# First batch of a Fourier filter followed by an MLP mixer: length-47 steps as four 64x64 tiles, results put back and transposed on chip

## The chip, the cores and the metric

The kernel runs on one core of a Trainium2 chip. The metric is the device time of one execution in microseconds (us). Engines are named as in the profile: PE is the matrix engine (PEld its weight loads), DVE the vector engine, ACT the scalar engine, POOL the GpSimd engine, SP the engine whose instruction queue only issues transfers here. ACT and POOL issue transfers too. Ln is line n of the kernel before unless the changed kernel is named.

## The reference, cut to what matters

```python
# x: (8, 3008, 256) f32; filt_r, filt_i: (1505, 256); weights arrive as 64-bit floats
X = np.fft.rfft(x, axis=1)
y = np.fft.irfft(X * (filt_r + 1j * filt_i)[None], n=3008, axis=1)      # "the filter"
h = np.maximum(y.transpose(0, 2, 1) @ w_tok1, 0) @ w_tok2               # 3008 -> 256 -> 3008
u = y + h.transpose(0, 2, 1)
out = u + np.maximum(u @ w_ch1, 0) @ w_ch2                              # 256 -> 1536 -> 256
```

## The kernel before, in words

**The transform.** 3008 is 47 x 64. A transform of the sequence is a length-64 step along one index (`wa`, a 128x128 matmul on 24 folded rows, `a_unit`, L533), a length-47 step for each of 32 frequencies k2 (`wb`, 96 rows in, 128 out), the product with the filter, the length-47 step back (`wi`) and the length-64 step back, which is part of the mixer's own matmul (`u_filter`, L872). Between the length-64 step and the length-47 step the data must be transposed: what lay on partitions (k2 and one of four parts g) has to lie in the free dimension, and the 24 rows a have to lie on partitions.

**The batches.** The eight batches are filtered one after the other, each beside the mixer of the batch before it, in steps placed by hand. Batches 1 to 7 transpose by writing to DRAM (`z_tmp`) and reading back, do the length-47 step as four 64x64 tiles of the PE array (`b_sets`, `bi_sets`, whose matmuls go through the helper `four`, L525), and write the result to DRAM again (`g_tmp`, L726), from which the mixer loads it (`t4_load`, L781). None of this has a mixer to lie beside in the first batch, so batch 0 is built otherwise:

- The length-64 step (12 matmuls, L535) is copied by ACT into one tile `turned`, a run of 256 channels for each of 32 places, and 16 DVE transposes in 32x32 blocks (L653), each over 16 channels, turn it in place. An element's neighbour in such a block lies 256 floats, 1 KB, further.
- For each of the 32 frequencies, `b_unit` (L666) does one 128x128 matmul of 256 columns whose stationary is every second column of a table (L668), DVE multiplies the result by the real and the imaginary part of the filter (L673), and `bi_unit` (L676) does two matmuls (L682). ACT copies the result out (L692) and writes it to `g_tmp` from its own queue (L689) for every second frequency. ACT also makes the second half of each filter tile (L253) and of each inverse table (L260, L261).
- The mixer's token product needs all of it: `t4_load` reads `g_tmp` back in pieces (L1270 to L1282, L784), and `token_sums` (L786) does 48 matmuls of 256 columns with the first mixer weight, which lies converted in `w1`.

**Weights beside it.** The weights are 64-bit floats and are converted on chip in tiles: 12 of the first mixer weight (0 to 11, 512 columns), 14 of the second (12 to 25, 470 columns, but 188 in tiles 18 and 25), then those of the channel weights (26 and on). For one tile ACT makes the top part (L281), DVE does four operations (L283 and L284, the first half, in `convert_middle`; L287 and L289, the second half, in `convert_end`), and top and rest are summed into place either by two PE matmuls and an ACT copy (L327, L328, L330: tiles 0 to 11, and the first `BY_PE` = 6 of the second weight) or by DVE (L316, the rest). Three scratch pairs are in use in turn, and `fill` keeps loads five tiles ahead. From step 27 of the 32 no new loads are started until the 32 steps are over (`pause`, L1262).

**Order.** The order on every engine is the order in which the program emits instructions; each engine works its own list in order. The main part (L1241 to L1301) emits the length-64 step, then the 32 steps with half a weight tile in each, so that 16 tiles are converted beside them, then the loads from `g_tmp`, then tiles 16 to 25 with `token_sums` in one piece after tile 17, then a ReLU (L866), two projections (`u_unit`, L879, each followed by a copy, L887) with tiles 26 and 27 beside them, and the sums of `v_steps` (L1298). Then the mixer's loop begins (`mix`, L1125). The channel weights' tile `both` (L1283) takes the memory of `turned`.

Of the kernel before, what the change touches and what calls it, by code (L numbers as in the profile page):

```python
# [37 lines left out]
WC = 2  # L38
TI = P - 2 * KH + 1
# [11 lines left out]
PARTS = (0, 64, 96, 112)  # L51
BY_PE = 6
# [7 lines left out]
def _make_tables():  # L60
# [12 lines left out]
    wa, wai = wa.reshape(P, P), wai.reshape(P, P)  # L73
# [25 lines left out]
    f = np.float32  # L99
    wi = wi.reshape(P, K2, KR)  # L100
    wa0 = wa.reshape(P, K2, 4).transpose(0, 2, 1).reshape(P, P)
    wbi0 = np.zeros((4, K2, K2, P + KR))
    wbi0[:, 0:A, :, 0:P] = wb
    wbi0 = wbi0.reshape(P, K2, P + KR)
    wbi0[:, :, P:] = wi
    places = np.zeros((P, K2, 2 * P))
    places[:, :, 0::2] = wbi0[:, :, 0:P]
    places[:, :, TI:TI + 2 * KR:2] = wbi0[:, :, P:]
    wbi0 = np.concatenate((places[one, :, 0:P], places[two, :, P:]))
    wbi0 = wbi0.reshape(P, K2 // WC, WC, P).transpose(0, 1, 3, 2)  # L110
# [18 lines left out]
def kernel(  # L129
# [26 lines left out]
                 for g, bs in enumerate(GROUPS)] for what, shape in (("z", (P, A)), ("g", (K2, KR))))  # L156
# [57 lines left out]
    turned = turned[:, 0:K2 * D].rearrange("p (s d) -> p s d", d=D)  # L214
# [7 lines left out]
    def filt_quad(c):  # L222
        t = filts[c % FB]
        for i, src in enumerate((filt_r, filt_i)):
            for odd in range(KC):
                k, to = c * KD + odd, odd * HALF
                nc.sync.dma_start(t[to:to + A, i], raw(src, k, [[64 * D, A], [KC * D, 2], [1, D]]))
                down = t[to + 32:to + 32 + A]
                if k:
                    nc.sync.dma_start(down[0:A - 1, i], raw(src, 64 - k, [[64 * D, A - 1], [-KC * D, 2], [1, D]]))  # L230
                else:
                    nc.sync.dma_start(down[:, i, 0], raw(src, 32, [[64 * D, A], [1, D]]))
                    nc.sync.dma_start(down[0:A - 1, i, 1], raw(src, 64 - KC, [[64 * D, A - 1], [1, D]]))

    def filt_load(c):
        t, k0 = filts_0[c % len(filts_0)], c * KC


        q = nc.gpsimd if c != 1 else nc.sync
        for src, i, p0 in ((filt_r, 0, 0), (filt_i, 1, 0)):  # L240
            q.dma_start(t[p0:p0 + A, i], raw(src, k0, [[64 * D, A], [D, KC], [1, D]]))
            lo = p0 + 32
            if k0 == 0:
                q.dma_start(t[lo:lo + A, i, 0, :], raw(src, 32, [[64 * D, A], [1, D]]))
            k = max(k0, 1)

            for j0, n in ((0, 16), (16, A - 1 - 16)):
                q.dma_start(t[lo + j0:lo + j0 + n, i, k - k0:KC, :],
                            raw(src, 64 * (j0 + 1) - k, [[64 * D, n], [-D, k0 + KC - k], [1, D]]))

    def filt_double(c):
        t = filts_0[c % len(filts_0)]
        nc.scalar.copy(out=t[HALF:P], in_=t[0:HALF])  # L253


    turn_i = sp.tile([P, 4, WC, KR], FP32, tag="s", name="turn_i")

    def table_turn(g, wb):
        wi, to = wb[:, TI:TI + 2 * KR:2].rearrange("p r k -> p k r"), turn_i[:, g % 4]
        nc.scalar.copy(out=to[0:HALF], in_=wi[HALF:P])  # L260
        nc.scalar.activation(out=to[HALF:P], in_=wi[0:HALF], func=AF.Copy, scale=-1.0)  # L261
# [40 lines left out]
    def rounded(st, n, parts, late):  # L302
        if late:

            late_in.reverse()
            where, tag = late_in[0]
            both = where.tile([P, 2, 512], FP32, tag=tag, name="both")
            pair = both[:, 0], both[:, 1]
        else:
            pair = spare_pair()  # L310
        h = halves(st, n, pair)
        yield next(h)
        yield next(h)
        top, rest = next(h)
        for src, dst in parts:
            nc.vector.tensor_tensor(out=dst, in0=src(top), in1=src(rest), op=ALU.add)  # L316
# [39 lines left out]
    def w2_load(i):  # L356
# [20 lines left out]
        else:  # L377
            yield from rounded(st, n, parts, False)
# [12 lines left out]
    def wc1_load(i, late=True):  # L391
# [6 lines left out]
        yield from rounded(st, 512, [(lambda v: v.rearrange("p (i j n) -> p i j n", j=2, n=P),  # L398
# [5 lines left out]
    def wc2_load(i):  # L404
# [8 lines left out]
        yield from rounded(st, 512, [(tile_of(dh), chan[1][:, i, n].rearrange("p j (g i) -> p j g i", i=CW))  # L413
# [47 lines left out]
    begun, pause = [0], []  # L461

    def fill(ahead):
        while not pause and begun[0] < len(tiles) and begun[0] < ended[0] + (4 if begun[0] >= len(tiles) - len(LAST) else ahead):
            start()
# [55 lines left out]
    def rows_of(t_d, b):  # L521
        g, i = place_of[b]
        return t_d[g].rearrange("k (g a) b d -> (k g) a b d", a=A)[:, :, i, :]

    def four(outs, stat, mov):  # L525
        for i in range(2):
            for j in range(2):
                nc.tensor.matmul(outs(i, j), stat(i, j), mov(i, j), start=True, stop=True)  # L528
# [4 lines left out]
    def a_unit(b, c):  # L533
        ps = bank(free_bank())
        nc.tensor.matmul(ps, wa0 if b == 0 else wa, xs.pop((b, c)).rearrange("p a d -> p (a d)"), start=True, stop=True)  # L535
        if b == 0:
            d0, c = divmod(c, NXC // 2)
            nc.scalar.copy(out=turned[:, ts(c, 2 * XC), ds(d0 * P, P)], in_=ps.rearrange("p (a d) -> p a d", d=P))
# [27 lines left out]
    def dft(bs):  # L566
# [5 lines left out]
        kept = []  # L572

        def table_load(c):
            if first:
                if c < 5:
                    where, tag = (t1p, "t1") if c > 2 else (wbp, "wb")
                    t = where.tile([P, 2 * P, WC], FP32, tag=tag, name="wb")
                    for h in range(2):
                        nc.gpsimd.memset(t[half_of(h), ts(1 - h, P)], 0.0)  # L580
                    kept.append(t)
                wbs[c] = kept[c % 5]
                for h in range(2):
                    nc.sync.dma_start(wbs[c][half_of(h), ts(h, P)], wbi0_d[half_of(h), c])
            else:
                wbs[c] = wbp.tile([P, 2, 4, HALF], FP32, tag="wb", name="wb")
                nc.sync.dma_start(wbs[c], wbi_d[:, ts(c, 2)])
# [4 lines left out]
        def w_load(c):  # L592
            table_load(c)
            (filt_load if first else filt_quad)(c)
# [45 lines left out]
        for i, u in enumerate(() if tiled else todo):  # L640
            if first and i in (0, 2):
                w_load(i // 2)
            if first and i in (6, 8):
                table_load(i // 2 - 1)
# [4 lines left out]
            if first and (i + 1) % (NXC // 2) == 0:  # L649

                for d in range(i // (NXC // 2) * P, (i + 1) // (NXC // 2) * P, 16):
                    v = turned.rearrange("p s d -> p d s")[:, d:d + 16, :]
                    nc.vector.transpose(v, v)  # L653
        t2s, t3s, prods = {}, {}, {}
# [11 lines left out]
        def b_unit(k):  # L666
            ps = bank("pg").rearrange("p (b d) -> p b d", b=2)[:, 0:nb, :]
            nc.tensor.matmul(ps, wbs[k // WC][:, 0:2 * P:2, k % WC], turned[:, k, :].unsqueeze(1), start=True, stop=True)  # L668
            t = filts_0[k // KC % len(filts_0)]
            if k == 0:  # L670
                prods["all"] = p1p.tile([P, 2, 2, D], FP32, tag="p1", name="p1")
            p1 = prods["all"][:, k % 2]
            nc.vector.tensor_tensor(out=p1, in0=ps.to_broadcast([P, 2, D]), in1=t[:, :, k % KC, :], op=ALU.mult)  # L673
            prods[k] = (p1[:, 0:1], p1[:, 1:2])

        def bi_unit(k):  # L676


            ps = bank(free_bank()).rearrange("p (b d) -> p b d", b=2)[:, 0:nb, :]
            for i, p in enumerate(prods.pop(k)):  # L680
                wi = turn_i[:, k // WC % 4, k % WC] if i else wbs[k // WC][:, TI:TI + 2 * KR:2, k % WC]
                nc.tensor.matmul(ps[0:KR], wi, p, start=(i == 0), stop=(i == 1))  # L682
            c, r = divmod(k, KC)
            if r == 0:
                where, tag = (p2p, "p2") if c % 3 == 2 else (t3p, "t3")
                t3s[c] = where.tile([KR, KC, nb, D], FP32, tag=tag, name="t3")
            by_block(t3s[c][:, r], ps[0:KR])
            if r == KC - 1:
                nc.scalar.dma_start(g_d[0][ts(c, KC)].rearrange("k r b d -> r k b d"), t3s.pop(c))  # L689

# [4 lines left out]
        def two_banks(tags):  # L695
            return [bank(tag).rearrange("p (j d) -> p j d", j=2) for tag in tags]

# [7 lines left out]
        def products(c, pss):  # L705
            where = (p1p, p2p)
            for h in range(2):
                prods[c, h] = where[h].tile([P, 2, 2, D], FP32, tag="p%d" % (h + 1), name="p%d" % (h + 1))
                nc.vector.tensor_tensor(out=prods[c, h], in0=pss[h].unsqueeze(1).to_broadcast([P, 2, 2, D]),
                                        in1=filts[c % FB], op=ALU.mult)  # L710
# [6 lines left out]
        def bi_sets(c, tags):  # L717
# [7 lines left out]
            for h in range(2):  # L725
                nc.sync.dma_start(g_d[place_of[bs[0]][0]][ts(c, KD), ts(h, KH)].rearrange("k r b d -> r k (b d)"),  # L726
                                    t3[half_of(h, KH)])
# [9 lines left out]
        yield "b"  # L737
        if not first:
            last = K2 // KD
# [13 lines left out]
        if first:  # L753
            for i in range(2):
                t = t2p.tile([P, 2, KC, D], FP32, tag="t2", name="filt")
                nc.gpsimd.memset(t[0:HALF], 0.0)
# [613 lines left out]
```

## Time and profile before

| | us |
|---|---|
| median of 3 runs (2404.61 to 2407.17) | 2407.01 |
| the profiled execution, its own time | 2404.98 |
| its span, first to last instruction | 2403.2 |
| last length-64 matmul's copy ends (ACT) | 21.5 |
| in-place transposes (L653) begin, end | 13.9, 31.1 |
| first product with the filter (L673) begins | 32.5 |
| last copy out of the length-47 step (L692) ends | 105.4 |
| token product (L790) begins, last matmul ends | 111.7, 132.7 |
| `v_steps` (L955 on `v`) begins | 139.7 |

What lies outside the span is 2404.98 - 2403.2 = 1.8 us. In the answers of the trace a row of groups has the line, the engine and operation, output<-input with shapes, the count, then the busy time and the mean of one in ns, then the idle time just before and what ended it. Each fp32 matmul has two records, so that x96 are 48 matmuls. In a table of stretches each engine has its busy time and (x) its records; then come the granted PE clock, the busy share of the 16 transfer engines, and what they moved in GB/s.

### The profile page before, as it was taken

The page shows a single profiled execution, that of the slowest core. Times are in us where ns is not written, and L with a number is a line of the kernel's source. Part 1 is how long each engine was busy: PE and PEld are TensorE (multiplying, and loading weights), DVE is VectorE, ACT ScalarE, POOL GpSimd, SP SyncE. Part 2 cuts the span into 40 slices and gives each one's busy share as a digit, 9 for nine tenths or more (in the row PEclk, how much of TensorE's full clock was granted, in tenths as well). Part 3 has the DMA queues.
Part 4 walks back from the last instruction along what each step waited for, and adds up shares of the span by engine and source line. Part 5 has one row for each costly group of instructions (what it writes and reads, how often), then busy time and mean ns, then how long its engine had stood idle before and what let it go on. Part 6 is the DMA issues. An engine that isn't in the chain of part 4 may idle for free.

```text
span 2403.2 us, 37053 instructions
## 1 busy us (share of the span) xinstructions
PE 2359.4 (98%) x13132; PEld 2012.9 (84%) x13132; DVE 1951.0 (81%) x3669; ACT 689.8 (29%) x1339; POOL 638.3 (27%) x1124
## 2 busy tenths in 40 slices
PE   7989999999999999999999999999999999999998
PEld 4667888888898888988888888988889888898887
DVE  7798887788887888788887788778887788877786
ACT  5732222222223222232222222222222322212222
POOL 7477434211211121112112311221121112112121
PEclk8999999999999999999999999999999999999999
DMA  9963546333353333533344333533335433331100
GB/s 218 241 195 121 152 119 226 114 118 85 106 188 124 100 95 117 189 118 96 98 145 158 117 93 103 186 120 107 90 114 172 132 98 98 108 130 32 39 14 21
DMA packets 189719, 294.28 MB, mean 122 GB/s; under 512 B 34444, under 2 KB 124962, under 8 KB 189534
## 3 DMA queue, kind: packets, MB, share of 16 engines
q1 hardware_dynamic: 148046, 231.24, 31.0%
q0 software_dynamic: 34688, 53.83, 8.6%
q10 hardware_dynamic: 6800, 6.85, 0.9%
q8 instruction: 104, 1.70, 0.3%
q14 instruction: 81, 0.66, 0.1%
HBM read 209.06 MB, written 82.72 MB: 121 GB/s over the span
## 4 chain that ended last, share of the span: by engine, by line
PE 92%; DVE 3%; DMA 2%; issue 1%; POOL 1%; ACT 1%; SPq 0%; ACTq 0%; DVEq 0%; POOLq 0%
PE ps_po L1011 35%; PE ps_pg L977 20%; PE ps_pg L993 15%; PE ps_b L528 3%; PE ps_b L841 3%; PE ps_acc L898 3%; PE ps_acc L841 2%; PE ps_pg L528 2%; PE ps_b L898 2%; PE ps_b L876 2%; PE ps_acc L876 2%; DVE both L284 0%; DVE t L955 0%; DMA g_tmp<-t 0%; DVE both L289 0%
## 5 line engine op out<-in xcount | busy, mean ns | idle before, releaser
L1019 POOL DMA_DIRECT2D out_dram<-r x752 | 408.3, 550 | 1452.0 <-issue 1028.0
L998 ACT ACTIVATE hh<-hh 128x512 f32<-128x512 f32 (+1 forms) x576 | 348.0, 621 | 1017.7 <-DVE hh L955 1013.8
L955 DVE TENSOR_TENSOR hh<-ps_pg,s 128x512 f32<-128x512 f32 (+3 forms) x864 | 482.5, 586 | 171.3 <-ACT s L980 161.1
L1011 PE MATMUL ps_po<-t,wc 128*128 128x256 f32 (+1 forms) x2296 | 558.1, 380 | 0.7 <-DVE t L955 0.7
L1011 PEld LDWEIGHTS ps_po<-t,wc 128*128 128x128 f32 x2296 | 427.7, 190 | 95.6 <-issue 38.7
L977 PE MATMUL ps_pg<-v,wc 128*128 128x256 f32 (+1 forms) x1728 | 412.6, 375 | 1.4 <-POOL wc L386 1.4
L1011 PE MATMUL ps_po<-hh,wc 128*128 128x256 f32 (+1 forms) x1722 | 411.5, 375 | 0.6 <-POOL wc L387 0.6
L977 PEld LDWEIGHTS ps_pg<-v,wc 128*128 128x128 f32 x1728 | 327.9, 190 | 39.6 <-POOL wc L386 2.2
L1011 PEld LDWEIGHTS ps_po<-hh,wc 128*128 128x128 f32 x1722 | 326.8, 190 | 38.4 <-POOL wc L387 1.4
L993 PE MATMUL ps_pg<-u,wc 128*128 128x256 f32 (+1 forms) x1152 | 292.3, 376 | 5.7 <-DVE hh L955 5.6
L955 DVE TENSOR_TENSOR t<-t,hh 128x256 f32<-128x256 f32 (+1 forms) x576 | 247.1, 429 | 19.8
L993 PEld LDWEIGHTS ps_pg<-u,wc 128*128 128x128 f32 x1152 | 217.2, 190 | 37.1 <-DVE hh L955 10.8
L955 DVE TENSOR_TENSOR s<-ps_pg,hh 128x512 f32<-128x512 f32 (+1 forms) x288 | 196.1, 681 | 30.0
L980 ACT COPY s<-ps_pg 128x256 f32<-128x256 f32 (+1 forms) x288 | 105.8, 368 | 332.4 <-PE ps_pg L977 329.1
L955 DVE TENSOR_TENSOR t<-hh 128x512 f32<-128x512 f32 (+1 forms) x288 | 194.4, 675 | 0.6 <-ACT hh L998 0.6
L977 PE MATMUL ps_pg<-u,wc 128*128 128x256 f32 (+1 forms) x576 | 169.3, 376 | 3.9 <-DVE hh L955 3.9
L993 PE MATMUL ps_pg<-v,wc 128*128 128x256 f32 (+1 forms) x576 | 169.2, 375 | 0.0
L977 PEld LDWEIGHTS ps_pg<-u,wc 128*128 128x128 f32 x576 | 108.1, 190 | 19.7 <-DVE hh L955 7.5
L993 PEld LDWEIGHTS ps_pg<-v,wc 128*128 128x128 f32 x576 | 109.2, 190 | 13.0
L955 DVE TENSOR_TENSOR u<-ps_acc,u 128x256 f32<-128x256 f32 (+1 forms) x84 | 46.2, 550 | 72.4 <-PE ps_acc L898 50.1
L955 DVE TENSOR_TENSOR u<-ps_b,u 128x512 f32<-128x512 f32 (+2 forms) x126 | 74.5, 591 | 28.8 <-PE ps_b L898 26.7
L898 PE MATMUL ps_acc<-w 128*128 128x256 f32 (+1 forms) x336 | 85.2, 376 | 0.0
(164 smaller groups left out, 2686.8 us busy)
## 6 DMA issues: line engine op xcount, KB each, us to landing
w<-w_tmp SPq DMA_DIRECT2D x84, 448.0 KB
w<-w_tmp SPq DMA_DIRECT2D x35, 896.0 KB
out_dram<-r POOLq DMA_DIRECT2D x696, 32.0 KB, 3.4
g_tmp<-t SPq DMA_DIRECT2D x112, 192.0 KB
t<-g_tmp SPq DMA_DIRECT2D x42, 512.0 KB
t<-z_tmp SPq DMA_DIRECT2D x196, 96.0 KB
z_tmp<-t SPq DMA_DIRECT2D x72, 256.0 KB
wb<-wbi_t SPq DMA_DIRECT2D x56, 256.0 KB
```

Of the source, the lines that this page charges most:

```text
L528: nc.tensor.matmul(outs(i, j), stat(i, j), mov(i, j), start=True, stop=True)
L841: nc.tensor.matmul(ps[:, at], w[:, n], mov, start=(j == 0 and i in (0, 2)), stop=(j == AP - 1 and i >= 5))
L876: nc.tensor.matmul(ps[:, ds(q * P, n)], t4[b, c][:, r, ts(dh, P)], wai[:, 0:n], start=(first and q == 0), stop=(not first and q == 3))
L898: nc.tensor.matmul(ps[:, ds(j * hw, hw)], h1[:, n, :], w2m[m % 2][:, at, 0:hw], start=(i < 2 and j == 0), stop=(j == len(todo) - 1))
L955: nc.vector.tensor_tensor(out=out, in0=in0, in1=in1, op=op)
L977: nc.tensor.matmul(ps[:, 0:hw], chan[0][:, jp, n, :], mov, start=True, stop=True)
L980: nc.scalar.copy(out=s[:, 0], in_=g[0][:, 0, 0:hw])
L993: nc.tensor.matmul(ps[:, 0:hw], chan[0][:, jp, n, :], mov, start=True, stop=True)
L998: nc.scalar.activation(out=hs, in_=hs, func=AF.Relu)
L1011: nc.tensor.matmul(po[i][:, j, 0:hw], chan[1][:, jp, n, :], mov, start=(jp == 0 and first == 1), stop=(jp == JP - 1 and last == 1))
L1019: q.dma_start(bass.AP(tensor=ob.tensor, offset=ob.offset + row * D + g * cw, ap=[[N1 * D, 32], [D if h else -D, n], [1, cw]]), blocks[ts(g ...
```

## The change

It touches the first batch, the tables, and one layout in DRAM.

- `turned` holds for each pair of neighbouring channels the 32 places, two channels in each (`TR` = 2): a run is 8 bytes, the next channel pair lies 256 bytes further, the next place 8 bytes. 16 transposes of 512 columns become 8 of 1024 (`turn_back`).
- Batch 0 uses `four`: per round of four frequencies `b_turned` has 8 matmuls of 64x64 that read `turned` directly, `products` 2 DVE operations of 1024 columns, and `bi_turned` 16 matmuls of 64x64. ACT makes one negated table per round, and copies the results with 4 copies back into `turned`, at the places where the input was. No filter tile and no inverse table is made by ACT any more. Filter loads are those of the other batches, real parts on SP, imaginary parts on POOL.
- After the eight rounds `turned` is transposed a second time by 8 more DVE operations. The token product reads `turned` directly, as 96 matmuls of 128 columns in four parts, one after each of the conversions of tiles 16 to 19. Six ACT copies (`t4_copy`) of 1024 columns put the data into the `t4` tiles, two after each of tiles 20, 21 and 22. There is no `g_tmp` for batch 0.
- `BY_PE` is 10: tiles 12 to 21 are summed by PE and ACT, 22 to 25 by DVE. The pause in the loads is gone. `both` is created after the copies.
- `g_tmp` of the other batches has its parts outermost, and each of their stores is four transfers of 24 rows in place of two of 48.
- Four small constant tables are loaded from SP in the third round and no longer from ACT before the rounds.

```diff
-BY_PE = 6
+TR = 2
+BY_PE = 10
 ...
-    turned = turned[:, 0:K2 * D].rearrange("p (s d) -> p s d", d=D)
+    turned = turned[:, 0:K2 * D].rearrange("p (q s r) -> p q s r", s=K2, r=TR)
 ...
+    def negate(c, wb):
+        nc.scalar.activation(out=negs[:, c % 4], in_=wb[:, :, 2], func=AF.Copy, scale=-1.0)
 ...
+    def turn_back(half):
+        for q in range(half * HALF, (half + 1) * HALF, CW):
+            for r in range(TR):
+                part = turned[:, q:q + CW, :, r]
+                nc.vector.transpose(part, part)
 ...
-            nc.scalar.copy(out=turned[:, ts(c, 2 * XC), ds(d0 * P, P)], in_=ps.rearrange("p (a d) -> p a d", d=P))
+            nc.scalar.copy(out=turned[:, ts(d0, HALF), ts(c, 2 * XC), :],
+                           in_=ps.rearrange("p (a q r) -> p q a r", q=HALF, r=TR))
 ...
+        def b_turned(c):
+            pss, wb = two_banks(turn), wbs[c]
+            for j in range(2):
+                four(lambda h, i: pss[h][half_of(i), j].rearrange("p (q r) -> p q r", r=TR), lambda h, i: wb[half_of(h), j, i],
+                     lambda h, i: turned[half_of(h), :, c * KD + j * KC + i, :])
+            return pss
+
+        def bi_turned(c):
+            pss, wb, neg = two_banks(("pg", "pg")), wbs[c], negs[:, c % 4]
+            p1, p2 = (prods.pop((c, h)) for h in range(2))
+            for j in range(2):
+                four(lambda i, h: pss[i][half_of(h), j], lambda i, h: wb[half_of(i), j, 2 + h],
+                     lambda i, h: p1[half_of(i), h, j], stop=False)
+                four(lambda i, h: pss[i][half_of(h), j], lambda i, h: wb[half_of(i), j, 3] if h else neg[half_of(i), j],
+                     lambda i, h: p2[half_of(i), 1 - h, j], start=False)
+            to = turned.rearrange("p (e g i) s r -> p g e i s r", e=DH, i=CW // TR)
+            for j in range(2):
+                for i in range(KC):
+                    nc.scalar.copy(out=to[:, :, :, :, c * KD + j * KC + i],
+                                   in_=pss[i][:, j].rearrange("p (g e i r) -> p g e i r", e=DH, i=CW // TR, r=TR))
 ...
-            for h in range(2):
-                nc.sync.dma_start(g_d[place_of[bs[0]][0]][ts(c, KD), ts(h, KH)].rearrange("k r b d -> r k (b d)"),
-                                    t3[half_of(h, KH)])
+            for g in range(4):
+                nc.sync.dma_start(g_d[place_of[bs[0]][0]][g, ts(c, KD)].rearrange("k a b d -> a k (b d)"),
+                                  t3[ds(g // 2 * HALF + g % 2 * A, A)])
 ...
+        filt_next(1)
+        negate(0, wbs[0])
+        filt_next(2)
+        pss = b_turned(0)
+        for c in range(last):
+            products(c, pss, tiles)
+            if c + 1 < last:
+                pss = b_turned(c + 1)
+            bi_turned(c)
+            yield
+            filt_next(c + 3)
+            yield
+            if c + 2 < last:
+                table_load(c + 2)
+            yield
+            if c + 1 < last:
+                negate(c + 1, wbs[c + 1])
+            yield
 ...
+    def t4_copy(c):
+        t4[0, c] = t4p.tile([P, TC4, D], FP32, tag="t4", name="t4")
+        nc.scalar.copy(out=t4[0, c].rearrange("p s (q r) -> p s q r", r=TR),
+                       in_=turned[:, :, ts(c, TC4), :].rearrange("p q s r -> p s q r"))
+
+    def token_sums(acc, e, part):
+        for a in range(part * AP, (part + 1) * AP):
             for t in range(TC):
-                nc.tensor.matmul(acc[:, t, :], w1[:, a, ts(t, P)], t4[b, a // TC4][:, a % TC4, :],
-                                 start=(a == 0 and t == 0), stop=(a == A - 1 and t == TC - 1))
-        return acc
+                nc.tensor.matmul(acc[:, t, ts(e, P)].rearrange("p (q r) -> p q r", r=TR), w1[:, a, ts(t, P)],
+                                 turned[:, ts(e, HALF), a, :], start=(e == 0 and a == 0 and t == 0),
+                                 stop=(e == 1 and a == A - 1 and t == TC - 1))
 ...
-        for c in range(A // TC4):
-            t4_load(0, c, PARTS[3], P, (nc.sync, nc.gpsimd)[c % 2])
-        both = wcp.tile([P, 2, JP, 7, P], FP32, tag="wc", name="wc")
-
-        chan.extend((both[:, 0], both[:, 1]))
+        acc = bank(free_bank()).rearrange("p (t d) -> p t d", t=TC)
+        parts = [(e, part) for e in range(DH) for part in range(2)]
+        for e in range(DH):
+            turn_back(e)
+        convert_middle()
+        fill(5)
         next(second)
         for i in range(IN_B, A // 2 + TC * W2G):
             convert()
-            if i == A // 2 + BY_PE - 1:
-                sum_up()
-                acc = token_sums(0)
+            if parts:
+                token_sums(acc, *parts.pop(0))
+            elif A // TC4 > len(t4):
+                t4_copy(len(t4))
+                t4_copy(len(t4))
+        sum_up()
+        both = wcp.tile([P, 2, JP, 7, P], FP32, tag="wc", name="wc")
+        chan.extend((both[:, 0], both[:, 1]))
```

## The prediction

> **What bounds the kernel now.** I read the page's busy slices first, then a table by stage, then the PE's order in one stage, then groups by form.
>
> ```profile
> 0.00:31.20 31.20, 13.52 (x24) 4.65 (x24) 21.70 (x20) 11.70 (x18) 24.32 (x50) 0.86 0.93 207
> 31.20:105.50 74.30, 72.77 (x255) 53.46 (x256) 54.96 (x99) 61.40 (x111) 46.13 (x85) 0.97 0.94 241
> 105.50:139.70 34.20, 31.40 (x133) 23.24 (x132) 29.58 (x67) 11.10 (x21) 19.62 (x37) 1.00 0.82 221
> 139.70:200.00 60.30, 52.29 (x208) 36.91 (x208) 55.84 (x100) 22.41 (x41) 48.21 (x78) 1.00 0.56 176
> 200.00:2403.00 2203.00, 2189.41 (x12516) 1894.63 (x12515) 1788.96 (x3386) 583.24 (x1149) 499.98 (x876) 1.00 0.37 114
> ```
>
> (Columns: stretch, its length, busy PE, PEld, DVE, ACT, POOL, granted clock, transfer share, GB/s.) From 200 us on PE is busy 99.4% of the time. Before that, the first batch is filtered and the weights are converted; only there can the change act on the end. The head has four stages: loading and transposing to 31.2; the 32 length-47 steps to 105.5, where PE is full and the transfers are at 94%; the way through DRAM, token product and last conversions to 139.7; then a stretch full on DVE. The length-47 stage on PE:
>
> ```profile
> 68.38 1.02 PE L328 MATMUL ps_po<-both,wai_t 128*128 128x512 f32 x2
> 69.24 0.61 PE L668 MATMUL ps_pg<-turned,wb 128*128 128x256 f32 x2
> 69.68 0.59 PE L682 MATMUL ps_b<-p,wb 128*96 128x256 f32 x2
> 70.11 0.59 PE L682 MATMUL ps_b<-p,turn_i 128*96 128x256 f32 x2
> 70.55 0.63 PE L668 MATMUL ps_pg<-turned,wb 128*128 128x256 f32 x2
> 71.01 0.59 PE L682 MATMUL ps_acc<-p,wb 128*96 128x256 f32 x2
> 71.44 0.59 PE L682 MATMUL ps_acc<-p,turn_i 128*96 128x256 f32 x2
> 71.87 1.02 PE L327 MATMUL ps_po<-both,wai_t 128*128 128x512 f32 x2
> 72.73 1.02 PE L328 MATMUL ps_po<-both,wai_t 128*128 128x512 f32 x2
> ```
>
> Starts are back to back: 4.35 us for two frequencies and one weight tile, 8.7 for four.
>
> **The change, part by part.** All sums stand against the profiled execution (2404.98 us); it is 2.0 below the median of 2407.01, to which I add the difference.
>
> *First transposes.* Now 16 of 1180 ns and 512 columns; then 8 of 1024.
>
> ```profile
> L653 DVE STREAM_TRANSPOSE turned<-turned 128x512 f32<-128x512 f32 x16 | 17.2, 1180 | 7.7 <-ACT turned L538 7.7
> L1090 DVE STREAM_TRANSPOSE r<-u 128x512 f32<-128x512 f32 x80 | 51.8, 685 | 0.0
> L668 PEld LDWEIGHTS ps_pg<-turned,wb 128*128 128x128 f32 x64 | 18.7, 314 | 17.5 <-issue 11.1 <-PE ps_po L327 3.5
> L790 PEld LDWEIGHTS ps_b<-t,w 128*128 128x128 f32 x96 | 18.2, 190 | 4.9 <-ACT both L281 2.4
> L330 ACT COPY w<-ps_po 128x240 f32<-128x240 f32 x6 | 3.5, 588 | 3.4 <-PE ps_po L328 2.2 <-ACT t L692 0.8 <-PE ps_b L682 0.4
> L980 ACT COPY s<-ps_pg 128x256 f32<-128x256 f32 x240 | 89.3, 372 | 304.7 <-PE ps_pg L977 301.5 <-DMA z_tmp<-t 1.9 <-ACT t L544 1.2
> ```
>
> A transpose with 1 KB steps takes 1180 ns where a dense one takes 685; an ACT copy that writes with 512-byte steps 588 for 240 columns where 256 dense ones take 372. The Trainium skill ("SBUF — State Buffer", section "Door 1: The DMA port swizzle") has a rule for it: memory is read in 16-byte lines, and two accesses to a line are enough for full speed. The change makes every step hit a line twice. By the rule a transpose of 1024 costs what the dense product of 1024 does (L709 follows itself after 1.14 us); by the strided row 2.3. I take 1.14. The last ACT copy still ends at 21.5, four transposes end at 26.1 in place of 31.1. The first product came 1.4 later, so it comes at 27.5 in place of 32.5.
>
> *The rounds.* Per four frequencies DVE has two products, 2 x 1.14 = 2.3, and two tiles at 2.25 (L283 to L283 with nothing between), 6.8 in all. PE: in later batches 8 small-tile matmuls take 0.9 us (241.60 to 242.51) and the next 8, with the change back to the full array, 1.2 (to 243.71); so 0.9 + 2.1 + four weight matmuls of 0.86 = 6.4, 6.7 with changes of tiling. ACT goes from 8.3 (four copies 1.5, two filter halves 2.1, four table halves 2.2, two L281 and two L330 2.5) to some 4.5. Transfers: filters 0.38 MB, table 0.26, two weight tiles 1.05, 1.7 MB, at 241 GB/s 6.9 us. Four limits within 0.5 us; I take 6.9 in place of 8.7. Eight rounds put the last products at 27.5 + 7 x 6.9 = 75.8. Transfers begin behind: input, four filter sets, six weight tiles and three tables are 8.8 MB, of which 6.4 are in at 31.2 us, so the third table lands at about 41; about 1.3 us of wait: 77.1. Then products 2.3, weight matmuls ahead in PE's queue 1.2, the inverse 2.1, four copies 1.6 (a copy of 256 into 8-byte runs: 0.39; with one access to a line 0.62, and 0.9 more): the last result is in place at 84.4 in place of 105.4. **21 us are gained here.** The negated table (0.3 per round) is hidden in ACT's idle time; without it, the inverse would wait those 0.3.
>
> *Behind the rounds.* Removed: the way from the last copy to the first token matmul, 111.7 - 105.4 = 6.3 us. Added: 8 transposes, 9.1 us, on the DVE that has the conversions. And the token product is cut into four parts that stand in PE's queue between tiles 16 to 19. ACT's copy of tile 16 stands before the first half of tile 19, that of 17 before 20, 18 before 21, 19 before 22; so **each of these DVE tiles waits for a part of the token product.** Nothing of this kind stands in the trace of before, where DVE runs ahead of PE. A part is 24 matmuls of 128 columns; 48 of 256 took 21.0, so a part takes 5.25 if its 8-byte runs cost nothing. PE's reads with steps: the only row is L668's weights, with 8-byte steps and thus two accesses to a line, and 314 ns where dense ones take 190. There the rule and the row part: by the rule a part is 5.25, by the row x1.65 = 8.7. PE wants a column in 0.84 ns (430 ns for 512), so a line for two in 1.7; ACT's 588 ns are 1.8 ns per line, the strided transpose's 2.0 (less some 0.16 fixed). The estimate from these is x1.15, 6.0. Now along the chain from 84.4: four transposes, 89.0; part 0, 95.0; tile 16 is later, since DVE has eight transposes (93.5), two first halves and a second half, 3.2: 96.7. Its matmuls 1.6, part 1 6.0, tile 17 1.6, part 2 6.0, tile 18 0.65, part 3 6.0, tile 19 1.6: 120.1. ACT's copy of 19 and L281 of 22: 1.8, 121.9. DVE then has what is left of tiles 20 to 26 up to the merge of 25: 12.8 by the rows (first halves 1.03 to 1.1, second halves 1.1, merges 0.85), and waits some 2.5 for ACT, which has six copies of 1024 (1.05 each; L253 took 1043 ns for as many dense ones) among the L281: 137.2. Two projections 5.2, copy and hand-over 0.8: **`v_steps` at 143.2 in place of 139.7, +3.5 us.**
>
> *The rest.* Stores of `g_tmp` are 112 more on SP at 0.38 us, in 2000 us; SP waits 484 us for ACT at this line, and PE waits for no load after 210: nothing (if a load did come late, some tenths for each batch; no gain). The A-stage copy with 32-byte runs hides behind the input loads (PE waits for these; uncovered 0.1 to 0.5). Fewer POOL issues, four constants moved past SP's third round: 0. Stage 139.7 to 200 is DVE work that stays.
>
> **Rivals.** (1) *The gain is given back in the queue*, as summed: 2404.98 + 3.5, by the median 2410.5. (2) *Faster*: the chain is as above without the stride's price (-2.1) and without late tables (-1.7), and the stage behind gains, since 6.3 MB less have to be moved in the head, 26 us of transfers at 241 GB/s: DVE idles 4.5 us from 139.7 to 200, with ACT waiting 4.0 for a channel weight's load. All of it: 2407.0 - 0.3 - 4.5 = 2402.2, and some lower if ACT's copies are cheaper. For: transfers at 0.82 before 139.7. Against: DVE is busy 93% there. (3) *Slower*: PE's reads of 8-byte runs cost what L668's weight load shows. The parts take 8.7, 3 x 2.7 more on the chain and the rounds 0.6 more: 143.2 + 8.5, 2419. It decides from about x1.22 on, where +3.5 becomes +4.8. (4) *Transposes stay slow*, the strided row holding for them too: 9.3 more behind the rounds, 4.6 before them: 2424; unlikely, since DVE's L284 reads with 8-byte steps at 692 ns for 512 columns, no more than a dense 687.
>
> **How the numbers follow.** 0.2% is 4.8 us, about what a measurement of this kernel can tell from no change. (1) 0.44, (2) 0.19, (3) and smaller excesses of the same kind, late filters among them, 0.31, (4) 0.06. The likeliest gives 2410.5, within 0.2%: 2402.2 to 2411.8. Within 0.2% 0.43, slower 0.38, faster 0.19. The range, 2400 to 2421, takes in (2) and (3) and leaves (4) and a still larger gain out.
>
> **What would show it.** L653's counterpart near 1.2 us for 1024 columns, else (4). Eight rounds of 6.9 us with the last copy into `turned` near 84; more means transfers. Four parts of the token product of 5.3 to 6 us with DVE idle 2 to 6 us before the first half of tiles 19 to 22, ended by ACT: the heart of it. If DVE doesn't wait there, I am wrong on the low side; `v_steps` at or after 150 would be (3). If `v_steps` is near 143 but the time isn't up by 3.5, the stage behind it has changed.

## The result, and the profile after

The changed kernel takes 2449.3 us (median of 4 runs, 2447.3 to 2449.5) against 2405.8 us for the kernel before on the same chip (2403.4 to 2407.2). The ratio is 1.018, with a 95% interval of 1.0162 to 1.0198: 43.5 us slower. The forecast was 2410.5 us with a range of 2400 to 2421, so the time lies outside it. The profiled execution has a span of 2447.7 us, 44.5 more than before.

The table by stage, with the stretches and columns of the kernel before's:

```profile
0.00:31.20 31.20, 16.03 (x40) 5.51 (x40) 16.11 (x14) 8.90 (x14) 19.30 (x31) 0.87 0.90 190
31.20:105.50 74.30, 33.76 (x244) 18.07 (x248) 31.93 (x49) 15.19 (x38) 20.48 (x26) 0.71 0.66 160
105.50:139.70 34.20, 32.55 (x245) 18.16 (x237) 29.32 (x41) 16.82 (x41) 2.16 (x4) 0.96 0.22 66
139.70:200.00 60.30, 45.25 (x232) 32.47 (x233) 41.16 (x83) 23.36 (x42) 31.80 (x58) 0.89 0.51 141
200.00:2447.00 2247.00, 2230.31 (x12685) 1924.66 (x12684) 1828.43 (x3461) 600.08 (x1179) 535.54 (x929) 1.00 0.37 115
```

The second row is the one to look at. In the stretch where PE had been full (72.8 of 74.3 us), it is busy for 33.8; DVE, ACT and POOL are idle for more than half of it too, and the transfers have fallen from 0.94 and 241 GB/s to 0.66 and 160. Nothing is full, so something is waited for in a row. The granted clock has fallen to 0.71 from 0.97 in this stretch, in which PE is idle for 40.5 us; whether the clock lengthens single matmuls there is not shown, and the waits below do not end on a matmul. Three landmarks say where the time goes: the last copy into `turned` ends at 129.3 us (forecast 84.4), `v_steps` begins at 184.8 (forecast 143.2, before 139.7), and 44.5 us of span are left of these 45.1.

What PE waits for in the rounds (its timeline; start, length, engine, line, operation, and in brackets the idle time ahead and what ended it):

```profile
37.74 0.69 PE L505 MATMUL ps_acc<-turned,wb 64*64 64x256 f32 x2 [9.70 <-DMA wb<-wbi_t]
63.68 0.69 PE L505 MATMUL ps_acc<-turned,wb 64*64 64x256 f32 x2 [18.36 <-DMA wb<-wbi_t]
```

The tables are late: over the rounds PE waits 43.7 us for five of them. Between the two lines it is DVE that is held, 12.3 us for a filter of the second set, whose product starts at 49.0. A table is 0.26 MB, 1.1 us at the 241 GB/s of the kernel before, so the next view is SP's queue, which issues it. The same stretch on SP:

```profile
39.19 3.13 SPq L227 DMA_DIRECT2D filt<-in_filt_r_dram  x1
42.36 0.61 SPq L230 DMA_DIRECT2D filt<-in_filt_r_dram  x1
43.01 2.33 SPq L227 DMA_DIRECT2D filt<-in_filt_r_dram  x1
...
48.25 2.21 SPq L227 DMA_DIRECT2D filt<-in_filt_r_dram  x1
50.51 0.26 SPq L230 DMA_DIRECT2D filt<-in_filt_r_dram  x1
...
53.24 0.59 SPq L560 DMA_DIRECT2D wb<-wbi_t  x1
```

SP needs 17 us (33.6 to 50.8) for twelve filter issues of 0.23 to 3.13 us each and the waits between them, and the next table is issued at 53.2. From one pair to the next it takes 3.0 us (39.19 to 48.25 for three). While it does so, the DMA engines are busy for a third of the time:

```profile
38.00:50.00 12.00, 7.32 (x52) 3.70 (x47) 1.00 (x1) 3.11 (x8) 6.25 (x7) 0.77 0.33 81
```

A transfer share of 0.33 and issues that take seven to ten times as long as others point to a narrow place inside the transfers. L227 loads 24 rows, L230 the 23 rows of the mirrored frequencies. In the kernel before, POOL issued nearly all of both, and the latter in pieces of 16 and 7 rows.

### The profile page after: what moved, and what is told of

It is laid out like the page before. It is cut to its first block, busy times and chain, and to the rows that moved or that the text cites. A ratio compares the mean times of both kernels' runs of the same rounds, so it can differ in the third digit from the quotient of the medians.

```text
span 2447.7 us, 37536 instructions
## 1 busy us (share of the span) xinstructions
PE 2357.9 (96%) x13436; PEld 1998.9 (82%) x13436; DVE 1946.9 (80%) x3645; ACT 664.4 (27%) x1313; POOL 609.3 (25%) x1047
## 4 chain that ended last, share of the span: by engine, by line
PE 90%; DVE 4%; issue 1%; ACT 0%; DMA 0%; POOL 0%; DVEq 0%; POOLq 0%; ACTq 0%
PE ps_po L986 35%; PE ps_pg L952 19%; PE ps_pg L968 15%; PE ps_b L505 3%; PE ps_b L816 3%; PE ps_acc L873 3%; PE ps_acc L816 2%; PE ps_b L873 2%; PE ps_pg L505 2%; PE ps_b L851 2%; PE ps_acc L851 2%; PE ps_b L765 1%; DVE t L930 1%; DVE both L261 0%; DVE hh L930 0%
## 5 line engine op out<-in xcount | busy, mean ns | idle before, releaser
L930 DVE TENSOR_TENSOR t<-t,hh 128x256 f32<-128x256 f32 (+1 forms) x576 | 245.9, 427 | 19.8
L676 DVE TENSOR_TENSOR p<-ps_acc,filt 128x1024 f32<-128x1024 f32 x64 | 77.7, 1214 | 33.9 <-PE ps_b L505 21.6
```

The source lines that it names most:

```text
L930: nc.vector.tensor_tensor(out=out, in0=in0, in1=in1, op=op)
```

## The experiments

Unless said otherwise, an experiment is the changed kernel with the edit shown. All 16 results, each against the kernel before beside it:

| run | median us | ratio to before, 95% interval |
|---|---|---|
| e1_split | 2431.5 | 1.0112 (1.0096 to 1.0127) |
| e2_no23 | 2423.2 | 1.0075 (1.0060 to 1.0090) |
| e3_no24 | 2442.5 | 1.0156 (1.0141 to 1.0171) |
| e4_pool | 2427.2 | 1.0092 (1.0075 to 1.0109) |
| e5_pool_split | 2422.4 | 1.0073 (1.0058 to 1.0088) |
| e6_tables | 2442.7 | 1.0158 (1.0143 to 1.0173) |
| e7_split_tables | 2424.4 | 1.0083 (1.0066 to 1.0100) |
| e8_pool_split_tables | 2424.1 | 1.0079 (1.0064 to 1.0094) |
| f1_order | 2439.9 | 1.0149 (1.0134 to 1.0164) |
| f2_order_pool_split | 2413.9 | 1.0038 (1.0023 to 1.0053) |
| f3_no_filters | 2409.0 | 1.0016 (1.0009 to 1.0023) |
| f4_before_runs | 2403.9 | 0.9996 (0.9987 to 1.0004) |
| g1_rows22 | 2431.0 | 1.0111 (1.0094 to 1.0128) |
| g2_rows19 | 2442.7 | 1.0158 (1.0142 to 1.0173) |
| g3_both_queues | 2417.9 | 1.0057 (1.0042 to 1.0072) |
| g4_before_cut | 2404.2 | 0.9996 (0.9988 to 1.0005) |

### Which transfers: the 23 rows, the 24 rows, or their number

Theory A: few of the 16 DMA engines carry a transfer of 23 rows, perhaps one. It is a rule of the Trainium skill ("DMA: Bandwidth & Descriptors", section "Why a DMA increments its semaphore by 16 and not by 1"): a transfer is spread over the largest number of engines up to 16 that divides the outermost size of both its sides, and the page's own example is 127 partitions, which go over one. By it 24 rows would have 12 engines and 23 rows, a prime, one. The page adds an exception: some copies that POOL issues are dealt out to 16 engines though 16 does not divide their row count. Theory B: SP's queue has eight places, so that each transfer waits until the eighth before it has landed, and many small ones use these places up.

**Cut in two, as before** (e1_split):

```diff
-q.dma_start(down[0:A - 1, i], raw(src, 64 - k, [[64 * D, A - 1], [-KC * D, 2], [1, D]]))
+for j, n in ((0, 16), (16, 7)):
+    q.dma_start(down[j:j + n, i], raw(src, 64 * (j + 1) - k, [[64 * D, n], [-KC * D, 2], [1, D]]))
```

> Sets 1 to 7 of the first batch's filters: each transfer of 23 rows is cut into one of 16 rows and one of 7, as the kernel before had them; same bytes, same queues, and four more transfers per set. Theory A (a transfer of 23 rows is carried by few of the 16 DMA engines, perhaps by one, and that engine sets the pace of the rounds): rounds of 7 to 9 us in place of 13.5, the last copy into `turned` near 85 to 95 us, and a time of 2404 to 2415 us. Theory B (eight transfers of SP's queue can be under way, each new one waits for the eighth before it, and small transfers use these places up): half as many filter transfers again, so rounds no shorter than 13.5 us; 2449 us or more, up to 2470.

Measured 2431.5, a gain of 17.8 us with half as many filter transfers again. Theory B alone, which had it no faster, falls; theory A gets about half of the smallest gain that it promised (34 us). PE still waited 27.2 us for four tables.

**Leave out one or the other** (e2_no23, and its mirror image e3_no24):

```diff
-                if k:
+                if k and left_out:
+                    pass
+                elif k:
                     q.dma_start(down[0:A - 1, i], ...
```

> Leaves out the 23-row transfers of sets 1 to 7 of the first batch's filters (the rows of the negative frequencies stay as they were, so the products of the first batch are not the reference's); the 24-row ones stay. Theory A: all of the delay goes, 2402 to 2412 us. Theory B: half of the small transfers and half of their bytes go, so about half of the delay does: 2422 to 2435 us.

> The mirror image: leaves out the 24-row transfers of the same sets (the positive frequencies' rows stay as they were, so the first batch's products are not the reference's) and keeps the 23-row ones; the same number of transfers and nearly the same bytes go as in the run without the 23-row ones. Theory A: the delay stays, 2438 to 2450 us. Theory B: as in the other, 2422 to 2435 us.

Measured 2423.2 and 2442.5. Almost the same bytes and the same number of transfers are left out, and one is worth 26.1 us, the other 6.8. Theory B had the two alike, so the 19.3 us between them speak for A. But e2_no23 lies in B's range and misses A's by 11 us, so the 23 rows are not all.

**All filters issued by POOL** (e4_pool):

```diff
-                filt_quad(c, tiles, (nc.sync, nc.gpsimd))
+                filt_quad(c, tiles, (nc.gpsimd, nc.gpsimd))
```

> Both halves of sets 1 to 7 are issued by POOL, as in the kernel before; the 23-row transfers stay whole. SP's queue then holds tables and weight tiles only. If the stall is one of SP's queue (theory B, or theory A where only SP's transfers are confined to one engine), the tables are in time: 2405 to 2420 us. If a 23-row transfer is as slow from POOL and the filters themselves come late: 2425 to 2450 us, with DVE's products waiting for filters in place of PE waiting for tables.

2427.2: the second case, at its good end. PE's waits for tables fall from 43.7 to 15.4 us, and DVE's products now wait 14.8 us for filters.

### Is the rest the tables' place in the queue?

e5_pool_split joins the last two edits (POOL alone, rows cut). The other three ask for the tables one round earlier, in the changed kernel (e6_tables), with the cut (e7_split_tables), and with cut and POOL (e8_pool_split_tables):

```diff
-            if first and i == 6:
-                table_load(1)
+            if first and i in (3, 6):
+                table_load(i // 3)
...
-            if c + 2 < last:
-                table_load(c + 2)
+            if c + 3 < last:
+                table_load(c + 3)
```

> Filter sets 1 to 7 issued by POOL alone, and their 23-row transfers cut into 16 and 7. With the 23 rows whole, POOL's filters still came late (products waited 7.3 us for one set) beside 15 us of waits for the first two tables. Theory A (few engines carry 23 rows, whichever queue issues it): the filter waits go, the table waits stay; 2412 to 2422 us. If POOL's waits were its issue time (12 issues of 0.55 to 1.1 us per set), the cut makes it worse: 2427 to 2440 us.

> The changed kernel with only its tables asked for one round earlier (table 1 at the fourth input chunk, table 2 at the seventh, then c + 3 in round c); filters whole and on both queues. PE waited 43.7 us for tables in the changed kernel. Theory Q (the tables are late because of their place in SP's queue): most of it goes, 2408 to 2420 us. Theory A (SP's queue is held by the filter transfers, and DVE's products wait for the filters instead): only the first of these waits goes, some 10 us: 2436 to 2446 us.

> The cut into 16 and 7 rows on both queues, and the tables one round earlier. With the cut alone PE still waited 27 us for four tables. If these waits are what is left of the loss: 2404 to 2412 us. If the SP queue's count of transfers is what is left, the waits move to the filters: 2422 to 2432 us.

> All three: filters from POOL alone, 23 rows cut into 16 and 7, tables one round earlier. If the three together are the whole of what kept the rounds from the 6.9 us that I had summed, the rounds go at 7 to 8 us, the last copy into `turned` ends near 85 to 90 us and the time is 2400 to 2412 us. If the volume of transfers bounds the stage as well, 2415 to 2425 us.

Measured 2422.4 (0.4 above theory A's range), 2442.7, 2424.4 and 2424.1. With POOL alone the cut is worth 4.8 us (2427.2 to 2422.4), against 17.8 where SP issues half of the filters. Earlier tables alone are worth 6.6 us; theory Q, that the tables were late only for their place in the queue, falls, since SP is held by what stands ahead of them. With e2_no23, four different mends now stopped between 2422 and 2424, all with the last copy into `turned` near 101 to 104 us. The three edits together (e8_pool_split_tables) are not the whole.

### The order behind the rounds

In all of these runs 55 to 57 us lie between the last copy and `v_steps`, as in the changed kernel (55.5), where the kernel before had 34.4. DVE in the changed kernel, in that stretch:

```profile
144.06 0.41 DVE L260 TENSOR_SCALAR both<-both 128x470 uint32<-128x470 uint32 x1 [1.02 <-ACT both L258]
...
151.00 0.41 DVE L260 TENSOR_SCALAR both<-both 128x470 uint32<-128x470 uint32 x1 [5.29 <-ACT both L258]
...
156.52 0.41 DVE L260 TENSOR_SCALAR both<-both 128x470 uint32<-128x470 uint32 x1 [3.43 <-ACT both L258]
...
163.93 0.41 DVE L260 TENSOR_SCALAR both<-both 128x470 uint32<-128x470 uint32 x1 [5.32 <-ACT both L258]
```

These are the waits that the prediction had called the heart of it: first halves, ended by ACT, one for each part of the token product; the fourth, of 5.3 us, ends at 163.9. f1_order moves the parts:

```diff
-            if parts:
+            if i == IN_B:
                 token_sums(acc, *parts.pop(0))
-            elif A // TC4 > len(t4):
+            elif i == A // 2 + BY_PE:
+                while parts:
+                    token_sums(acc, *parts.pop(0))
+            elif i > A // 2 + BY_PE and A // TC4 > len(t4):
```

> The changed kernel with one thing altered: parts 1 to 3 of its first token product no longer stand in PE's queue behind tiles 17, 18 and 19, but together behind tile 21, the last that PE converts (part 0 stays where it is); the copies of `turned` for the filter follow three steps later. DVE idled 1.0, 5.3, 3.4, 5.3 and 1.2 us before first halves in the changed kernel, each ended by ACT. If these waits come from the parts in PE's queue, as the prediction had it, 8 to 13 of the 16 us go: 2436 to 2442 us, with 43 to 48 us in place of 55.5 from the last copy into `turned` to `v_steps`. If the block of three parts is then the last thing that the projection waits for: no gain, 2447 to 2452.

2439.9, a gain of 9.5 us, and 47.1 us from the last copy (130.1) to `v_steps` (177.3). In it, the first of these waits, the next one before a first half, and the longest of all:

```profile
144.89 0.41 DVE L260 TENSOR_SCALAR both<-both 128x470 uint32<-128x470 uint32 x1 [1.01 <-ACT both L258]
...
151.15 0.41 DVE L260 TENSOR_SCALAR both<-both 128x470 uint32<-128x470 uint32 x1 [0.58 <-ACT both L258]
...
170.53 0.69 DVE L293 TENSOR_TENSOR wc<-both 128x512 f32<-128x512 f32 x1 [4.36 <-PE ps_b L765]
```

The waits of 5.3, 3.4 and 5.3 are gone; a new one of 4.4 stands at the end, for the three parts at once, whose last one frees the buffer that the channel weights are written to. f2_order_pool_split has this order on top of e5_pool_split:

> The same order, with filter sets 1 to 7 from POOL and 23 rows cut into 16 and 7 (2422.4 us without the new order). If the two losses are independent, as the nearly equal 55 to 57 us from the last copy to `v_steps` in all runs so far say: 2409 to 2415 us.

2413.9, 8.5 us under e5_pool_split: the two losses add up. It is the fastest form of the change that I found, and still 0.4% behind the kernel before.

### Without filters

f3_no_filters is e5_pool_split with `filt_next` emptied:

```diff
-            if c < last:
+            if c < 0:
                 filt_quad(c, tiles, ...
```

> Leaves out every filter transfer of sets 1 to 7 of the first batch (its products are then those of set 0 and of zeroed or old tiles, not the reference's), with tables and weights as in the changed kernel. Four different mends of the filters and tables all stopped at 2422 to 2424 us with rounds of some 9.5 us. If the filters' own volume or count is the floor: rounds near 7 us, last copy near 85, 2404 to 2410 us. If the weight tiles and tables are: 2416 to 2424 us.

2409.0. Its DVE timeline, the first product of three rounds, and the projection's first step:

```profile
45.33 1.22 DVE L677 TENSOR_TENSOR p<-ps_acc,filt 128x1024 f32<-128x1024 f32 x1
53.02 1.22 DVE L677 TENSOR_TENSOR p<-ps_acc,filt 128x1024 f32<-128x1024 f32 x1
...
80.32 1.22 DVE L677 TENSOR_TENSOR p<-ps_acc,filt 128x1024 f32<-128x1024 f32 x1
...
143.36 0.69 DVE L931 TENSOR_TENSOR v<-u 128x512 f32<-128x512 f32 x1 [2.22 <-ACT u L863]
```

Five rounds from 45.33 to 80.32 are 7.0 us each (7.4 over all seven, with 7.7 us of waits for the first two tables), the last copy ends at 86.7 and `v_steps` begins at 143.4. The prediction had 6.9, 84.4, 143.2 and a time of 2410.5. So the forecast is that of the changed kernel with filters that cost nothing, and 40.4 of the 43.5 us are the filters' (2449.31 - 2408.95).

### One part of the change in the kernel before

f4_before_runs gives the kernel before the runs of two channels alone (`turned` as `"p (q s r) -> p q s r"`, the ACT copy, 8 transposes of 1024 and the length-47 product's operand to match):

```diff
-            nc.tensor.matmul(ps, wbs[k // WC][:, 0:2 * P:2, k % WC], turned[:, k, :].unsqueeze(1), ...
+            nc.tensor.matmul(ps[:, 0].rearrange("p (q r) -> p q r", r=2), wbs[k // WC][:, 0:2 * P:2, k % WC], turned[:, :, k, :], ...
```

> The kernel before with one part of the change alone: `turned` in runs of two channels, so the ACT copy writes 8-byte runs, 8 transposes of 1024 take the place of 16 of 512, and the length-47 products read 8-byte runs. The first product can begin some 5 us sooner (27.5 us). If PE's full queue sets the pace of the stage behind it: 2400 to 2403 us. If the transfers do (94% busy there): 2404 to 2407 us, no change.

2403.9, between the two ranges, with an interval that holds 1: no change that can be measured. The first product came 3.0 us sooner (29.55; it then waited for ACT's copy of the filter), the last result 2.6 and `v_steps` 0.7. From 31.2 to 85 us, in the kernel before and in this run:

```profile
31.20:85.00 53.80, 53.77 (x190) 39.99 (x191) 40.74 (x72) 43.92 (x79) 41.79 (x78) 0.95 0.93 233
31.20:85.00 53.80, 53.80 (x192) 40.05 (x191) 40.60 (x73) 46.35 (x82) 42.90 (x79) 0.97 0.99 247
```

Transfers rose from 0.93 to 0.99, and PE is busy for all of the 53.8 us in both. That fits the second case, but the run does not tell which of the two sets the pace.

### Why 23 rows are slow

> The changed kernel, with 22 of the 23 rows of each such transfer of sets 1 to 7 loaded (row 23 is left as it was, so those products are not the reference's); same queues, same number of transfers, 4% fewer bytes in them. Theory A (23 rows have no divisor up to 16 but 1, and one engine carries them; 22 go over 11): the loss of the 23 rows goes, 2423 to 2433 us. Theory S (small transfers are slow whatever their rows): 2445 to 2450 us.

> The same with 19 of the 23 rows, 17% fewer bytes and fewer rows than the run with 22 (four rows are left as they were, so those products are not the reference's). Theory A: 19 has no divisor up to 16 but 1 either, so 19/23 of the 26 us stay: 2440 to 2448 us, slower than with 22 rows. Theory S: no slower than with 22 rows.

```diff
-q.dma_start(down[0:A - 1, i], raw(src, 64 - k, [[64 * D, A - 1], [-KC * D, 2], [1, D]]))
+q.dma_start(down[0:n, i], raw(src, 64 - k, [[64 * D, n], [-KC * D, 2], [1, D]]))     # n = 22, n = 19
```

22 rows take 2431.0 us and 19 rows, with fewer bytes, 2442.7, both inside theory A's ranges. That can't be volume, number, queue or order: all are the same or speak for 19. That any odd number of rows is slow these two runs don't exclude; the cut into 16 and 7, at 2431.5 as fast as 22 rows, speaks against it. With 22 rows SP's issues in the first sets go like this (timeline of g1_rows22):

```profile
39.07 0.30 SPq L227 DMA_DIRECT2D filt<-in_filt_r_dram  x1
40.01 0.29 SPq L231 DMA_DIRECT2D filt<-in_filt_r_dram  x1
41.08 0.30 SPq L227 DMA_DIRECT2D filt<-in_filt_r_dram  x1
```

No issue takes over 0.35 us, and the twelve are out in 9.0 us (34.4 to 43.5) in place of 17. With 19 they take 14.5 (33.0 to 47.5), single ones up to 1.8:

```profile
38.84 1.79 SPq L227 DMA_DIRECT2D filt<-in_filt_r_dram  x1
...
43.52 1.77 SPq L227 DMA_DIRECT2D filt<-in_filt_r_dram  x1
```

Other transfers suffer with them: between 30 and 130 us POOL's weight tiles of 470 KB need 11.6 us (median) from issue to landing with 23 rows, 10.5 with 19, 4.8 with 22 and 6.2 with 16 and 7. The runs agree with the skill's rule in both directions (22 = 2 x 11; 19 and 23 are prime). The pace fits too: a pair is 46 KB for one engine and a twelfth of 48 KB, 50 KB in 3.0 us, by the rule an estimate of 17 GB/s for that engine, and a sixteenth of the 241 GB/s of the kernel before is 15. No view here shows the single engines, so "one engine" is what rule, row counts and pace agree on, and not itself shown.

Last, two attempts at a faster version: g3_both_queues is f2_order_pool_split with the 24-row transfers issued by SP,

```diff
-                q.dma_start(t[to:to + A, i], raw(src, k, [[64 * D, A], [KC * D, 2], [1, D]]))
+                nc.sync.dma_start(t[to:to + A, i], raw(src, k, [[64 * D, A], [KC * D, 2], [1, D]]))
```

and g4_before_cut is f4_before_runs with the cut of e1_split in `filt_quad`, which batches 1 to 7 of the kernel before use with 23 rows whole.

> The version with the new order of the token product (2413.9 us), filters of sets 1 to 7 cut into 16 and 7 rows, but the 24-row transfers issued by SP and the cut ones by POOL, so that neither queue has 12 to a set. If POOL's eight places were what is left (rounds of 9.4 us where 6.9 go without filters): 2404 to 2410 us. If the filters then stand in SP's queue ahead of tables and weights, as in the changed kernel: 2412 to 2422 us.

> The kernel before with `turned` in runs of two channels (2403.9 us), and in batches 1 to 7 the 23-row filter transfers cut into 16 and 7. PE is busy 99% there and its loads are asked for some 60 us ahead, so one slow engine should cost nothing: 2402 to 2406 us. Under 2400 if something in the second batch waited for them after all.

2417.9 for the first: slower than with POOL alone, as PE waits 19.8 us for tables again. 2404.2 for the second, against 2403.9 without the cut: in batches 1 to 7, whose loads are asked for long ahead, the whole 23 rows cost nothing that can be measured. None of the 16 beats the kernel before beyond its interval.

## Why the prediction was wrong

The groups of the changed kernel in its first 200 us that answer to the prediction's steps (busy us and mean ns behind the bar):

```profile
L511 DVE STREAM_TRANSPOSE turned<-turned 128x1024 f32<-128x1024 f32 x16 | 18.4, 1212 | 10.5 <-ACT turned L521 10.5
L662 ACT COPY turned<-ps_pg 128x256 f32<-128x256 f32 x32 | 9.7, 393 | 60.0 <-PE ps_pg L505 51.3 <-issue 8.7
L765 PE MATMUL ps_b<-turned,w 128*128 128x128 f32 x192 | 22.2, 273 | 1.1 <-DVE turned L511 1.1
```

- *First transposes*: right. 1212 ns for 1024 columns (1.14 us taken), first product at 28.2 us (27.5). Two hits per line were enough on DVE, and rival (4) is out.
- *The rounds*: **the step that failed.** "Transfers: filters 0.38 MB, table 0.26, two weight tiles 1.05, 1.7 MB, at 241 GB/s 6.9 us" priced the filters by their bytes, at a rate measured on transfers of another shape and queue. A round took 13.5 us (first products at 28.2 and 122.9, seven rounds). The sum missed two lines of the diff: the cut into 16 and 7 rows was taken out, and half of the filter issues went from POOL to SP, ahead of tables and weights. "Fewer POOL issues ... 0" counted only what POOL lost. The limits of PE (6.7) and DVE (6.8) fit: without filters a round takes 7.0. ("Four limits within 0.5 us" is a slip, since ACT's was 4.5, and 1.7 MB at 241 GB/s are 7.0 us; neither moves the forecast by a microsecond or decides it.)
- *The last copy at 84.4, a gain of 21 us*: 129.3 in place of it, a loss of 24. Without filters 86.7.
- *Negated table hidden*: right in the main; its copy was what PE waited for in 1.6 us of the whole.
- *The token product's parts*: a part takes 5.53 us, x1.05 of 5.25, so the 8-byte runs cost no more than that in place of the x1.15 taken, far from the x1.65 of rival (3). The copies into 8-byte runs take 393 ns (0.39 taken).
- *DVE waits for a part at tiles 19 to 22*: right in place, and in size (2 to 6 us) but for the first: 1.0, 5.3, 3.4 and 5.3 us. From the last copy to `v_steps` 55.5 us (58.8 summed).
- *The stage behind*: right within 1 us. `v_steps` is 45.1 later, the span 44.5.
- *The rivals*: the result is on the side of (3), but by another mechanism, and 38.8 us above the forecast where (3) had 8.5. "Late filters among them" stood there as a smaller excess, with no price.

Of the 43.5 us, 18 are the number of rows as such: 17.8 by the cut (e1_split), 18.3 by 22 rows (g1_rows22). The 26.1 of e2_no23 hold half of the filters' bytes and issues as well. Another 9 go when the cut filters leave SP's queue for POOL's (2431.5 to 2422.4), and 13 are the filters in the best form of them that I tried (2422.4 against 2409.0). The last 3 to 4 are the prediction's own balance: the gain in the rounds, given back behind them.

The 13 have two main parts. Round by round, e5_pool_split loses 7.8 us on f3_no_filters in the first three rounds (28.6 to 61.0 against 28.5 to 53.0) and 4.8 in the last (83.25 to 94.61 against 73.77 to 80.32). The last round's loss is a weight tile that stands behind the filters in POOL's queue: POOL issues six such tiles from 87.7 us on, where the run without filters has them out from 51.6. ACT waits for the tile, and DVE for ACT:

```profile
91.82 0.62 ACT L259 ACTIVATE both<-st 128x470 f32<-128x470 f32 x1 [6.07 <-DMA st<-in_moe_w_tok_dram]
92.48 0.41 DVE L261 TENSOR_SCALAR both<-both 128x470 uint32<-128x470 uint32 x1 [4.73 <-ACT both L259]
```

What the first three rounds lose is **not settled**: transfers are at 1.07 between 40 and 50 us, which speaks for volume, and between 50 and 70 us at 0.71 to 0.86 with POOL waiting for its own earlier transfers (16.5 us over all rounds), which speaks for the number in flight. g3_both_queues, which shares them out, brought new waits for tables and doesn't tell the two apart.

## What to carry to other kernels

Price a transfer by its shape and queue, not by its bytes: look at the row count of each side first, and cut a row count that has no large divisor up to 16 (23 into 16 and 7 was worth 18 us here). When a diff joins transfers or moves them to another queue, list what stands behind them in that queue; a table of 0.26 MB was waited for 18 us because twelve small, slow filter transfers stood ahead of it, and a weight tile 6 us behind filters that were cut. And where the consumer is far behind, the same slow transfers cost nothing (batches 1 to 7), so it is a question of the stage and not of the instruction.

## What the runs showed of the hardware that was not expected

- A transfer of 22 rows instead of 19 made the kernel 11.7 us faster (2431.0 against 2442.7) with more bytes moved.
- The cost shows in the issuing engine as well: SP needed 2.1 to 3.1 us for four of six 24-row issues in a set between whole 23-row ones, and 0.30 us for all six between 22-row ones.
- PE read its moving operand in runs of 8 bytes with 256-byte steps at 5.53 us for a part's 48 matmul records of 128 columns: 5% over what dense rows of 256 columns give (20.96 us for 96 records in the kernel before, a quarter of it 5.24), with the price of the shorter matmuls in these 5%.
